# Packed copies of the leftover rows for four inverse transforms, and a new order of work

## The chip, the cores and the metric

One core of a Trainium2 chip runs the kernel as a single launch. The metric is the device time of one execution in microseconds (us). The core has five engines with instruction queues of their own: TensorE (PE in the profile, its weight loads PEld), VectorE (DVE), ScalarE (ACT), GpSimd (POOL) and SyncE (SP), which here issues nearly all DMAs. Queues run in order, and they wait for each other by semaphores.

## The reference

x has 2048 rows of 640 numbers in bf16. It is normalized by rows, and two branches are added to it: a two-dimensional Fourier filter, and a two-layer MLP with gelu.

```
xn = layernorm(x)                                  # (1, 2048, 640)
A  = irfft2(rfft2(xn) * (w_r + 1j * w_i))          # over rows and columns
h  = gelu(xn @ w1 + b1)                            # 640 -> 1536
B  = h @ w2 + b2                                   # 1536 -> 640
out = x + A + B
```

## The kernel before

The 2048 rows are 16 chunks (c = 0 to 15) of 128 rows; row p*16 + c is partition p of chunk c. The program first lists all steps with their buffers, and then places them by two texts written into the file: ORDER, which gives each step its engine and its place in that engine's queue, and SLOTS, which gives each buffer its slot. The method sync() derives the semaphore waits from the buffers. So the order is fixed ahead and nothing is decided on the chip. The first matmuls of the MLP and of the filter are mixed on TensorE, and the second MLP matmuls fill the places where the filter waits.

The steps, by the names in ORDER:

- Loads on SP: x0 to x14 (rows), w1_hj (ten pieces), w2_0 and w2_1 (halves of w2), W.. (sixteen large and two small pieces of the filter weights into the tile Wf, all on one semaphore), g, e, m, n, i, h (tables).
- Layernorm of chunk c: st, ag, then sq and rs or ve and rs, then nm, which writes the normalized chunk. sq uses a square root on ACT; table0 and table1 load the tables for the root and for gelu.
- Transposes into xnT: tp (TensorE) and tc (copy) for chunks 0 to 3, td (transposing DMA on SP) for the others. Chunk 0 is normalized in two parts, nm0 and nm0.3. b1mm and b1cp turn the bias b1 into a column.
- MLP, first layer: h{block}.{column block}.{first of the inner pieces}, gelu in ge. Second layer: k for chunks 1, 2, 4, 5, 7, 8, 10, 11, whose sum with x + b2 is put aside by kk; l for the others, which adds into the bank of the last step. xs adds b2 to x.
- Filter, way there: f1 and f2 fold the columns, G and gx transform over the rows (first half), b0 to b5 with xb transform over the columns (groups of 3, 3, 2, 3, 3 and 2), c with y finish the rows in 32x32 tiles, m and z multiply by the filter.
- Filter, way back: d and u (32x32 tiles), vt0 to vt15 (transposing DMAs on SP into XV), e0 to e5 (the same groups), yo, y2 and yf (unfolding), fin (last transform over the rows) and os (sum with what was put aside), out (stores).

A folded quarter of the columns has 160 rows here: 128, and 32 leftover. width() lists the matmuls of one group of n chunks: 4n with 128 rows of weights, then 4n with the 32 leftover rows of the four quarters, each in a row group of its own. In e0 to e5 the weights come from XV, 128 columns that lie 16 elements apart; in b0 to b5 they lie side by side. b, c, d and e all use PSUM banks 0 to 3, so that each of these groups waits until the one before it is copied out.

The lines of the profile: L410 is every matmul, L420 and L421 are copies on ACT and DVE, L405 loads, L559 td, L705 vt, L764 y2, L769 yf, L796 kk, L806 os, L813 out. The diff touches sync(), the tables of constants at L243 to L250, ORDER, SLOTS, the pools at L400 and the loop over the groups at L753.

Of the kernel before, what the change touches and what calls it, by code (L numbers as in the profile page):

```python
# [107 lines left out]
class Plan:  # L108
# [58 lines left out]
    def sync(self):  # L167
# [77 lines left out]
SUMS = 2  # L245
KEEP = (1, 2, 4, 5, 7, 8, 10, 11)
# [5 lines left out]
sp:x0 dve:warm0 act:bias1 pool:id0 pool:wpad dve:eps5 pool:id1 pe:idle0 sp:x1 act:table0 pool:xbpad2a pool:mhalf pool:xbpad0a pool:xbpad0b  # L252
pool:xbpad1b sp:w1_00 pool:xbpad1a pool:xbpad2b sp:w1_01 sp:w1_02 dve:st0.0 sp:x2 dve:st0.1 sp:w1_03 dve:st1.0 sp:w1_04 dve:ag0 dve:st1.1 sp:w1_10
act:sq0 dve:rs0 dve:ag1 sp:w1_11 dve:nm0 act:sq1 pe:b1mm dve:nm0.3 act:table1 sp:w1_12 dve:rs1 pe:tp0.3 dve:nm1 pe:tp0.0 sp:w1_13 pe:idle1 dve:tc0.0
pe:tp1.0 sp:w1_14 dve:f10.1 pe:h0.0.0 dve:f10.0 sp:x4 pe:h0.1.0 act:tc1.0 pe:h0.0.1 pe:h0.1.1 sp:x6 dve:f20.11 pe:h0.0.2 act:tc0.3 dve:f20.00
pe:h0.1.2 pe:h1.1.0 sp:g act:b1cp pe:h1.1.1 pe:h1.1.2 sp:x8 pe:h1.0.0 dve:st3.0 pe:h1.0.1 pe:h1.0.2 sp:x10 dve:st3.1 pe:h0.0.3 pe:h1.0.3 sp:x12
pe:h1.1.3 dve:ag3 dve:st2.0 pe:h0.0.4 pe:h0.1.3 dve:ve3 pe:h1.0.4 act:ge0.1 dve:st2.1 pe:h0.3.0 pool:rs3 pe:h1.1.4 act:ge1.0 pe:h0.2.0 dve:ag2
act:ge0.0 pe:h0.3.1 dve:ve2 pe:h0.1.4 act:ge1.4 dve:nm3 pe:h0.2.1 pool:rs2 pe:h0.2.2 act:ge0.3 dve:f20.10 pe:h1.3.0 act:ge1.1 pe:h1.3.1 dve:f20.01
pe:h0.3.2 act:ge1.2 dve:nm2 pe:tp3.0 pe:h1.3.2 dve:f11.0 pe:h1.3.3 act:tc3.0 pe:h1.3.4 dve:f11.1 pe:h0.3.3 pe:tp2.0 act:ge0.2 dve:st5.0 pe:h0.2.3
# [36 lines left out]
pe:h6.0.0 sp:vt12 act:ge6.10 pe:h6.0.3 pe:l3.0.6 act:ge6.0 pe:l3.384.0 pe:l3.384.3 pe:l3.384.6 pe:l3.384.9 pe:l0.0.0 pe:e0 pe:l0.0.3 act:yo0.0
dve:yo0.1 pe:l0.0.6 pe:l0.0.9 dve:y20.1 pe:e1 dve:y20.0 dve:yf0.0 pe:l0.384.0 act:yo1.0 pe:l0.384.3 dve:yf0.1 pe:l0.384.6 act:yo1.1 pe:l0.384.9
# [33 lines left out]
def bass_parallel_sum__spectral_gfnet__dense_activation_gelu__prompt_kernel(  # L331
# [20 lines left out]
    K = Plan(nc)  # L352
    with ExitStack() as es:
# [60 lines left out]
        def pe(name, lst, **kw):  # L414
            return K.op(name, "pe", mms(lst), **kw)
# [431 lines left out]
```

## Time and profile before

| what | value |
|---|---|
| three runs, median (lowest to highest) | 149.14 us (148.47 to 150.26) |
| the profiled execution, its own time | 148.87 us |
| its span, first to last instruction | 147.5 us |
| SP: issue of one transposing DMA into XV | 1.26 to 2.26 us |
| transposing DMA into XV, issue to landing | 2.6 to 4.5 us, median 2.8 |
| stores (160 KB), issue to landing | 1.8 us, median |
| HBM read and written | 10.92 MB and 2.62 MB |

What a run takes beyond its span, 1.37 us in the profiled one, lies before the first and after the last instruction. The profile gives busy times by engine and by line. A row of instructions has the engine, the line, the operation, the tile written and the tiles read, the shapes, the count, the total busy time, the mean in ns, and the idle time of the engine ahead of them with what ended it. A matmul's duration includes its way through the array, so the matmuls of one group overlap, and their durations add up to more than the group takes. A row of the timeline merges neighbouring instructions of the same form: start, length, engine, and the idle time ahead in brackets.

### The profile page before, as it was taken

Reading aid. Unit: us, or ns where it says so; the run is one execution under the profiler, and the core shown is the slowest. Engines: PE = TensorE matmul, PEld = TensorE weight load, DVE = VectorE, ACT = ScalarE, POOL = GpSimd, SP = SyncE. Lnnn points to the kernel's source line nnn. Section 1 sums busy time; section 2 is a strip of 40 time slices with the busy share of each in tenths; the row PEclk is TensorE's granted clock in tenths of the full one; section 3 lists DMA queues with packets and bytes.
Section 4 is the critical chain, followed back from the end, with each engine's and each line's share of the span. In section 5 each row is a group of like instructions: output and inputs, shape, how many; then the busy total and the mean of one; then the engine's idle time right before and its main releaser. Section 6 shows DMA issues by size and latency. Waiting matters only on the chain.

```text
span 147.5 us, 4149 instructions
## 1 busy us (share of the span) xinstructions
PE 141.7 (96%) x1751; PEld 99.8 (68%) x1760; DVE 114.7 (78%) x264; ACT 79.3 (54%) x149; POOL 7.2 (5%) x24
## 2 busy tenths in 40 slices
PE   7999999999999999999999999999899999999993
PEld 7899898886478867455364434446686786667882
DVE  2999999999997555798988999410488789296993
ACT  3659998979755734577795767655242102300000
POOL 2030204112000000000000000000000000000000
PEclk9999999999999999999999999999999999999999
DMA  4999869887999899000007685669001022012225
GB/s 135 306 354 408 142 141 343 145 101 137 293 155 160 221 201 266 16 4 0 7 0 57 126 118 99 103 131 94 2 0 49 0 78 102 5 44 89 89 93 178
DMA packets 29226, 18.40 MB, mean 125 GB/s; under 512 B 20248, under 2 KB 27928, under 8 KB 29080
## 3 DMA queue, kind: packets, MB, share of 16 engines
q1 hardware_dynamic: 29184, 18.14, 54.2%
q8 instruction: 14, 0.23, 0.6%
q14 instruction: 4, 0.03, 0.1%
q10 hardware_dynamic: 24, 0.00, 0.0%
HBM read 10.92 MB, written 2.62 MB: 92 GB/s over the span
## 4 chain that ended last, share of the span: by engine, by line
PE 86%; DMA 4%; ACT 3%; DVE 2%; SPq 2%; issue 1%
PE ps L410 85%; DMA XV<-U 2%; SPq L705 2%; ACT Xb L420 2%; DMA X<-in_A_x_dram 2%; DVE U L521 1%; ACT U L420 1%; PE ps L567 1%; ACT gT L639 0%; DVE T L553 0%; DVE W L806 0%; DVE mv L523 0%; DVE rstd L527 0%
## 5 line engine op out<-in xcount | busy, mean ns | idle before, releaser
L410 PE MATMUL ps<-W,gT 128*128 128x256 bf16 (+3 forms) x396 | 59.3, 296 | 0.0
L410 PE MATMUL ps<-xnT,W 128*128 128x256 bf16 (+2 forms) x411 | 55.5, 286 | 1.2 <-issue 1.1
L410 PEld LDWEIGHTS ps<-W,gT 128*128 128x128 bf16 x396 | 36.9, 98 | 15.4 <-issue 1.2
L410 PEld LDWEIGHTS ps<-xnT,W 128*128 128x128 bf16 x420 | 34.5, 98 | 16.0 <-issue 2.8
L639 ACT ACTIVATE gT<-ps,b1col 128x256 bf16<-128x256 f32 (+2 forms) x84 | 37.6, 524 | 10.3 <-PE ps L410 10.0
L420 ACT ACTIVATE Wf<-ps 128x960 bf16<-128x960 f32 (+1 forms) x8 | 6.7, 869 | 19.2 <-PE ps L410 15.7
L521 DVE BATCH_NORM_STATS2 U<-X 128x6 f32<-128x320 bf16 x32 | 14.1, 473 | 2.1 <-DMA X<-in_A_x_dram 2.1
L420 ACT ACTIVATE T<-ps 128x644 bf16<-128x644 f32 (+2 forms) x17 | 9.3, 580 | 4.7 <-PE ps L410 4.7
L796 DVE TENSOR_TENSOR xnT<-ps,X 128x384 f32<-128x384 f32 (+1 forms) x16 | 7.6, 486 | 4.8 <-PE ps L410 4.8
L806 DVE TENSOR_TENSOR W<-ps,xnT 128x384 bf16<-128x384 f32 (+1 forms) x16 | 7.5, 485 | 4.7 <-PE ps L410 4.5
L420 ACT ACTIVATE XV<-ps 128x1280 bf16<-128x1280 f32 (+1 forms) x8 | 9.6, 1202 | 2.0 <-PE ps L410 2.0
L421 DVE CAST Wf<-ps 128x960 bf16<-128x960 f32 (+1 forms) x4 | 4.3, 1073 | 7.1 <-PE ps L410 7.1
L584 DVE TENSOR_TENSOR T<-T 128x128 bf16<-128x128 bf16 (+1 forms) x32 | 8.9, 315 | 0.1
L806 DVE TENSOR_TENSOR W<-ps,X 128x384 bf16<-128x384 f32 (+3 forms) x17 | 7.6, 465 | 1.7 <-PE ps L410 1.6
L410 PE MATMUL ps<-Wf,htab 128*128 128x384 bf16 (+3 forms) x33 | 8.6, 296 | 0.0
L410 PE MATMUL ps<-getab,XV 32*128 32x160 bf16 (+1 forms) x128 | 7.5, 242 | 0.5 <-DMA XV<-U 0.5
L420 ACT ACTIVATE Xb<-ps 128x960 bf16<-128x960 f32 x5 | 6.2, 1260 | 3.4 <-PE ps L410 3.4
L410 PEld LDWEIGHTS ps<-getab,XV 32*128 32x128 bf16 (+1 forms) x128 | 6.7, 146 | 1.7 <-DMA XV<-U 0.8
L420 ACT ACTIVATE U<-ps 128x512 bf16<-128x512 f32 (+2 forms) x13 | 5.3, 475 | 4.4 <-PE ps L410 4.4
L699 DVE TENSOR_TENSOR T<-T 128x644 bf16<-128x644 bf16 x16 | 7.3, 487 | 0.2
L410 PE MATMUL ps<-EB,XV 32*128 32x160 bf16 (+1 forms) x128 | 7.2, 232 | 0.2 <-ACT Xb L420 0.2
L532 POOL TENSOR_TENSOR rstd<-ve,mhalf 128x2 f32<-128x2 f32 (+1 forms) x8 | 6.1, 758 | 26.6 <-DVE ve L531 26.6
(56 smaller groups left out, 124.6 us busy)
## 6 DMA issues: line engine op xcount, KB each, us to landing
out_dram<-W SPq DMA_DIRECT2D x15, 160.0 KB, 1.8
X<-in_A_x_dram SPq DMA_DIRECT2D x7, 320.0 KB, 5.8
W<-in_B_w_dram SPq DMA_DIRECT2D x10, 192.0 KB, 4.7
W<-in_B_w_dram SPq DMA_DIRECT2D x2, 960.0 KB, 7.0
Wf<-in_A_w_r_dram SPq DMA_DIRECT2D x7, 160.5 KB, 5.5
Wf<-in_A_w_i_dram SPq DMA_DIRECT2D x7, 160.5 KB, 3.8
gtab<-c_G SPq DMA_DIRECT2D x1, 512.0 KB, 7.5
htab<-c_H SPq DMA_DIRECT2D x1, 512.0 KB, 6.1
```

The lines of the kernel that those rows point to most:

```text
L410: ins = e.matmul(o_, lhsT=lw, rhs=rh, start=st, stop=sp_, skip_group_check=True)
L420: return e.activation(dst(), src(), ACT.Copy)
L421: return e.tensor_copy(dst(), src())
L521: K.op(f"st{c}.{h}", "dve", lambda e, _, c=c, h=h: e.bn_stats(stats[:, c, 6 * h:6 * h + 6], view(X, c * D + H2 * h, [[1, H2]])), reads=[B_ ...
L532: K.op(f"rs{c0}", "pool", lambda e, _, a=a, b=b: e.tensor_tensor(out=rstd[:, a:b], in0=ve[:, a:b], in1=mhalf[:, a:b], op=ALU.pow), reads=[ ...
L567: ins = e.transpose(psb(tps.slot, [[1, 512]]).bitcast(BF)[:, 128 * j:128 * j + 128], xnv(n, 128 * j, [[1, 128]]), ident)
L584: ring_ops.append(K.op(f"f2{pair}.{k}{i}", "dve", lambda e, _, op=op, x1v=x1v, xfv=xfv, o_=o_, o0=o0, o1=o1, w=w: e.tensor_tensor(out=xfv( ...
L639: K.op(f"ge{bi}.{fc}", "act", lambda e, _, c0=c0, nt=nt, fc=fc, f0=f0, hps=hps: e.activation(gT[:, fc, 128 * c0:128 * (c0 + nt)], psb(hps. ...
L699: return e.tensor_tensor(out=rows, in0=rows, in1=view(TT, TB.slot * 4 * KP + r * KP, [[2 * KP, 2], [1, KP]]), op=op)
L705: K.op(f"vt{q}", "sp", lambda e, _, q=q, qq=qq, U=Us[pair]: e.dma_start_transpose(XV[:, :, 128 * q:128 * q + 128], uv(U, D * qq, [[1, D]]) ...
L796: K.op(f"kk{c}.{o0}", "dve", lambda e, _, kps=kps, c=c, home=home, o0=o0, w=w: e.tensor_tensor(out=home[:, o0 // 128:(o0 + w) // 128], in0 ...
L806: K.op(f"os{c}.{o0}", "dve", lambda e, _, c=c, os_=os_, fps=fps, o0=o0, w=w, kept=kept, home=home if kept else None: e.tensor_tensor(out=( ...
```

## The change

Three things change. First, for the groups 2 to 5 (NEAR) a copy, xr, gathers the leftover rows of the group's n chunks out of XV into a tile T with the 128 columns side by side, and the leftover matmuls of e2 to e5 read their weights there. The copies are ready to run when the last vt has landed; xr2 and xr4 are placed on ACT, xr3 and xr5 on DVE. There are three slots; xr5 takes that of xr2 and so follows e2. The other e matmuls stay.

Second, a step no longer waits by semaphore for table0 or table1 when it runs on the same engine as they do.

Third, ORDER and SLOTS are new throughout. Steps change places in every queue, and some change engines: xb4.1 goes from ACT to DVE, gx7.0 and several y and yo from DVE to ACT. e2 and e3 change places: e0, e1, e2, e3, e4, e5 instead of e0, e1, e3, e2, e4, e5.

The sizes, the matmuls, the loads and the other copies are the same.

```diff
-            o.waits = [d for d in set(o.deps) if d.dma or d.eng != o.eng or o.eng != "pe"]
+            o.waits = [d for d in set(o.deps) if d.dma or d.eng != o.eng or o.eng != "pe" and d.name[:5] != "table"]
...
+NEAR = (2, 3, 4, 5)
...
-        p_yo, p_y2, p_yf, p_os = [Pool(k, n) for k, n in (("yo", 2), ("y2", 1), ("yf", 2), ("os", 4))]
+        p_yo, p_y2, p_yf, p_os, p_xr = [Pool(k, n) for k, n in (("yo", 2), ("y2", 1), ("yf", 2), ("os", 4), ("xr", 3))]
...
-            pe(f"e{gi}", lambda c0=c0, n=n, eps_=eps_: width(
-                eps_.slot, n, lambda i, g, p0, k: part(XV, p0, k, 2048 * g + c0 + i, [[16, 128]]), getab),
-                reads=B_v + [B_ge], writes=[eps_])
+            xr = K.buf(f"xr{gi}", p_xr) if gi in NEAR else None
+            if xr:
+                K.op(f"xr{gi}", "act dve", copy(lambda c0=c0, n=n, xr=xr: view(TT, 384 * xr.slot, [[128, n], [1, 128]]),
+                     lambda c0=c0, n=n: view(XV, 2048 * 4 + c0, [[1, n], [16, 128]])), reads=B_v, writes=[xr])
+            pe(f"e{gi}", lambda c0=c0, n=n, eps_=eps_, xr=xr: width(
+                eps_.slot, n, lambda i, g, p0, k: part(TT, p0, k, 384 * xr.slot + 128 * i, [[1, 128]]) if xr and g == 4 else part(XV, p0, k, 2048 * g + c0 + i, [[16, 128]]), getab),
+                reads=B_v + [B_ge] + ([xr] if xr else []), writes=[eps_])
```

Of ORDER, one queue at a time, the stretches that matter below (old, then new):

```
start, PE    old  b1mm tp0.3 tp0.0 idle1 tp1.0 h0.0.0 h0.1.0 h0.0.1 h0.1.1 h0.0.2 h0.1.2 h1.1.0
             new  tp0.3 b1mm tp0.0 idle1 tp1.0 h0.1.0 h0.1.1 h0.0.0 h0.0.1 h0.0.2 h1.0.0
start, ACT   old  sq1 table1 tc1.0 tc0.3 b1cp          new  sq1 table1 b1cp tc1.0 tc0.3
start, DVE   old  rs0 ag1 nm0 nm0.3 rs1 nm1            new  rs0 ag1 nm0.3 nm0 rs1 nm1
SP           old  td11 W12n bias2 W00m w2_1 W02p W02n e W01n td12 td14 td15 td13 W11p W03n W10p m ...
             new  td9 td8 bias2 w2_1 W11p W13n m W12p W03n W10m e W03p W10p W00p W02n W01n W12n W11n td12 td15 td14 td13 ...
PE           old  G10 h5.3.3 h5.1.0 h5.1.3 h4.8.0 h4.8.3 h4.9.0 k2.0.0 k2.0.3 k1.0.6
             new  h5.0.3 G11 h5.5.0 k1.0.6 k1.0.9 G10 k2.0.0
PE           old  b4 h5.6.0 h5.6.3 h5.7.0 h5.7.3 b3    new  b4 k4.0.0 k4.0.3 h5.6.0 b3
DVE          old  ... y2.0 m1.1 m1.0 z1.0 m0.1 z1.1 m0.0 m3.1 xb3.0
             new  ... y2.0 kk5.384 m1.1 m0.1 m1.0 z1.0 z1.1 xb4.1 m3.1 m0.0 xb3.0
ACT          old  u0.1 u1.1 ge5.10 u1.0 u2.0           new  u0.0 u1.0 ge5.11 u1.1 u0.1 u3.0
SP           old  vt2 vt3 vt1 vt7 vt0 vt6 vt4 vt5 vt8 vt9 vt11 vt10 vt14 vt15 vt13 vt12
             new  vt1 vt2 vt3 vt6 vt0 vt7 vt4 vt5 vt11 vt9 vt10 vt8 vt14 vt15 vt12 vt13
PE           old  d3.0 h6.4.0 h6.4.3 h6.10.0 h6.10.3 k8.0.9 l3.0.0 h6.11.0 h6.11.3 l3.0.3 h6.0.0 h6.0.3 l3.0.6
                  l3.384.0 l3.384.3 l3.384.6 l3.384.9 l0.0.0 e0
             new  d3.0 h6.11.3 h6.10.0 h6.8.0 h6.8.3 l3.0.0 h6.10.3 l3.0.3 l3.0.6 h6.0.0 l3.0.9 h6.4.0 h6.4.3 h6.0.3
                  l3.384.0 l3.384.3 l3.384.6 l0.0.0 e0
PE           old  e1 l0.384.0 .3 .6 .9 fin0.0 fin0.384 l3.0.9 e3 ...
             new  e1 l0.384.0 .3 .6 .9 fin0.384 l0.0.9 fin0.0 e2 k11.0.0 .3 .6 .9 l6.0.0 fin2.0 fin1.0 fin3.384 ...
DVE          new  xr3 yo0.1 y20.0 y20.1 yf0.1 yf0.0 os0.384 y21.1 y21.0 xr5 os0.0 yf1.0 yf1.1 kk11.0
ACT          new  ge6.0 xr2 yo0.0 xr4 yo1.0 yo1.1 yo2.0 yo2.1
```

More of the change, by code (lines that the diff above doesn't have):

```diff
@@ L251 @@
 ORDER = """
[L252 to L259, printed above, removed]
@@ new lines @@
+pe:h6.8.3 pe:l3.0.0 sp:vt15 act:ge6.8 pe:h6.10.3 act:ge6.11 pe:l3.0.3 act:ge6.10 sp:vt12 pe:l3.0.6 pe:h6.0.0 pe:l3.0.9 sp:vt13 pe:h6.4.0 pe:h6.4.3
+pe:h6.0.3 act:ge6.4 pe:l3.384.0 pe:l3.384.3 act:ge6.0 pe:l3.384.6 dve:xr3 act:xr2 pe:l0.0.0 pe:e0 pe:l0.0.3 dve:yo0.1 act:yo0.0 pe:l3.384.9 pe:l0.0.6
+act:xr4 dve:y20.0 pe:e1 dve:y20.1 pe:l0.384.0 dve:yf0.1 act:yo1.0 pe:l0.384.3 dve:yf0.0 pe:l0.384.6 act:yo1.1 pe:l0.384.9 pe:fin0.384 pe:l0.0.9
+dve:os0.384 pe:fin0.0 dve:y21.1 pe:e2 dve:y21.0 pe:k11.0.0 act:yo2.0 dve:xr5 pe:k11.0.3 dve:os0.0 act:yo2.1 pe:k11.0.6 dve:yf1.0 sp:out0.0 pe:k11.0.9
@@ new lines @@
+bps0:0 xb1:1 bps1:0 xb2:2 bps2:0 xb3:0 bps3:0 xb4:1 bps4:0 xb5:3 bps5:0 Y0:1 Y1:0 Y2:2 Y3:3 Y4:5 Y5:4 Y6:0 Y7:1 T0:1 T1:0 T2:1 T3:0 T4:0 T5:1 T6:0
+T7:1 U0:0 U1:1 U2:3 U3:2 U4:1 U5:0 U6:3 U7:2 cps0_0:0 cps0_1:0 dps0_0:0 dps0_1:0 cps1_0:0 cps1_1:0 dps1_0:0 dps1_1:0 cps2_0:0 cps2_1:0 dps2_0:0
+dps2_1:0 cps3_0:0 cps3_1:0 dps3_0:0 dps3_1:0 yo0:0 y20:0 yf0:0 eps0:0 os0:0 fps0_0:6 fps0_384:5 os1:2 kps1_0:4 kps1_384:5 fps1_0:1 fps1_384:4 os2:1
+kps2_0:6 kps2_384:7 fps2_0:0 fps2_384:7 yo1:1 y21:0 yf1:1 eps1:0 os3:0 fps3_0:4 fps3_384:7 os4:3 kps4_0:5 kps4_384:7 fps4_0:4 fps4_384:0 os5:0
@@ new lines @@
+kps5_0:6 kps5_384:5 fps5_0:1 fps5_384:7 yo2:0 y22:0 yf2:0 eps2:0 xr2:0 os6:2 fps6_0:6 fps6_384:6 os7:1 kps7_0:5 kps7_384:7 fps7_0:3 fps7_384:1 yo3:1
+y23:0 yf3:0 eps3:0 xr3:2 os8:3 kps8_0:6 kps8_384:7 fps8_0:2 fps8_384:6 os9:0 fps9_0:7 fps9_384:1 os10:1 kps10_0:5 kps10_384:6 fps10_0:5 fps10_384:5
+yo4:0 y24:0 yf4:1 eps4:0 xr4:1 os11:2 kps11_0:5 kps11_384:7 fps11_0:1 fps11_384:0 os12:0 fps12_0:2 fps12_384:0 os13:3 fps13_0:5 fps13_384:4 yo5:0
+y25:0 yf5:1 eps5:0 xr5:0 os14:2 fps14_0:3 fps14_384:4 os15:1 fps15_0:2 fps15_320:6 fps15_480:3
```

128 lines of the change are left out of this document (62 added, 66 removed).

## The prediction, made before the changed kernel was run

> **What bounds the kernel now.** I read the page first, then the busy time by stretches, then the chain of work in order of time.
>
> ```profile
> span 147.5 us, 4149 instructions
> ...
> PE 141.7 (96%) x1751; PEld 99.8 (68%) x1760; DVE 114.7 (78%) x264; ACT 79.3 (54%) x149; POOL 7.2 (5%) x24
> ```
>
> ```profile
> 5.60:60.00 54.40, 54.32 (x644) 43.64 (x646) 47.61 (x134) 41.04 (x84) 6.06 (x8) 1.00 0.94 220
> 60.00:103.90 43.90, 41.96 (x683) 21.11 (x688) 31.96 (x55) 29.36 (x55) 0.15 (x2) 1.00 0.43 62
> 103.90:145.00 41.10, 41.06 (x389) 30.96 (x389) 32.03 (x64) 6.74 (x8) 0.00 (x0) 1.00 0.15 54
> ```
>
> ```profile
> 100.19 3.65 DMA XV<-U
> ...
> 103.89 41.09 PE ps L410 x375
> ...
> 145.00 0.33 DVE W L806
> ```
>
> In the second fence the first number after the stretch is its length, then come the busy times of PE, PEld, DVE, ACT and POOL. TensorE is the bound: it is idle for 0.08 us between 5.6 and 60, for 1.94 us between 60 and 103.9, and for 0.04 us of the last 41. The granted clock is 1.00 throughout. So only three things can shorten the kernel: less TensorE time per matmul, less of those 1.94 us, or a shorter start or end. A new order alone can give little, and any wait it opens on TensorE is paid in full. The chain shows what starts the last stretch: the last transposing DMA of XV, landing at 103.84.
>
> **The change part by part.** *Leftover rows.* Each of the transforms e0 to e5 has 4n matmuls with 128 rows of XV as weights and 4n with 32 leftover rows (n chunks in the group). In both, 128 weight columns are read 16 elements apart. The transforms b0 to b5 have the same shapes with neighbouring columns, so they are the yardstick.
>
> ```profile
> L410 PEld LDWEIGHTS ps<-getab,XV 128*128 128x128 bf16 x64 | 5.1, 144 | 1.2 <-DMA XV<-U 0.8 <-ACT Wf L420 0.2
> ...
> L410 PE MATMUL ps<-getab,XV 32*128 32x160 bf16 x64 | 2.5, 250 | 0.0
> ...
> L410 PE MATMUL ps<-EB,XV 32*128 32x160 bf16 x64 | 2.2, 231 | 0.0
> ...
> L410 PEld LDWEIGHTS ps<-getab,XV 32*128 32x128 bf16 x64 | 1.6, 148 | 0.5
> ...
> L410 PEld LDWEIGHTS ps<-EB,XV 32*128 32x128 bf16 x64 | 1.0, 92 | 0.8
> ```
>
> ```profile
> 110.09 1.36 PE L410 MATMUL ps<-getab,XV 128*128 128x160 bf16 x24
> ```
>
> ```profile
> 125.27 1.02 PE L410 MATMUL ps<-getab,XV 128*128 128x160 bf16 x16
> ```
>
> ```profile
> 63.40 1.31 PE L410 MATMUL ps<-EB,XV 128*128 128x160 bf16 x24
> ```
>
> ```profile
> 81.74 0.96 PE L410 MATMUL ps<-EB,XV 128*128 128x160 bf16 x16
> ```
>
> A leftover load takes 148 ns strided and 92 ns packed. The change packs those of e2 to e5: 2+3+3+2 = 10 chunks, 40 loads. Were every load on TensorE's path, that would be 40 x 56 ns = 2.2 us; that is one end, and nothing is the other. The whole groups decide between them: 24 matmuls take 1.36 strided against 1.31 packed, 16 take 1.02 against 0.96. So one delay of about 0.05 us per group is visible, and the same for two chunks as for three; the rest lies behind running matmuls. Four groups x 0.05 = **-0.20 us**. The 128-row loads stay strided (144 ns).
>
> The Trainium skill (TensorE: Matmul & The Clock Gate, Part 3, The mechanism) says that a weight load overlaps running matmuls only where its row group differs. By that rule each later round of four leftover loads, which returns to the same row groups, would be exposed, so 1+2+2+1 = 6 rounds x 56 ns = 0.34 us would be gained instead of 0.20. The trace does not agree: three chunks lose no more than two.
>
> *The copies.* xr2 and xr4 go to ACT and xr3 and xr5 to DVE, 384 or 256 elements each, with a 16-element source step.
>
> ```profile
> L420 ACT ACTIVATE Wf<-ps 128x960 bf16<-128x960 f32 x5 | 4.7, 969 | 12.6 <-PE ps L410 12.6
> ...
> L764 DVE TENSOR_TENSOR Wf<-Wf 128x960 bf16<-128x960 bf16 x8 | 5.1, 652 | 0.1
> ...
> L806 DVE TENSOR_TENSOR W<-ps,xnT 128x384 bf16<-128x384 f32 x8 | 4.4, 551 | 2.8 <-PE ps L410 2.7
> ...
> L420 ACT ACTIVATE xnT<-ps 128x640 bf16<-128x640 bf16 x3 | 2.1, 703 | 0.3 <-PE ps L567 0.2
> ...
> L420 ACT ACTIVATE xnT<-ps 128x256 bf16<-128x256 bf16 x1 | 0.4, 378 | 0.0
> L421 DVE COPY xnT<-ps 128x384 bf16<-128x384 bf16 x1 | 0.4, 358 | 0.0
> ```
>
> No row copies with that step within SBUF; the nearest give 0.36 to 0.55 us on DVE and 0.38 to 0.70 on ACT, and I take 0.4 and 0.5. The Trainium skill (VectorE: DVE Perf Modes, the TRN2 errata) has (224 + 384)/1.2 GHz, an estimated 0.51 us, for ACT's larger one; no run here shows it. xr2 and xr3 run beside e0, xr4 behind yo0.0; ACT sat idle for 12.6 us before its Wf copies, so those cost nothing. xr5 is the tight one. It stands in DVE's queue ahead of os0.0, yf1.0 and yf1.1, and fin3.384 on TensorE waits for yf1.1. From the end of e1: two ACT copies (1.9), two y2 (1.3), xr5 (0.4), os0.0 (0.55), two yf (1.3), 5.5 us in all. TensorE's work there in the new order is four 256-column triples, e2, five 384-column triples, one more of these for l0.0.9, and four single matmuls: 1.3 + 1.0 + 2.4 + 0.5 + 0.6 = 5.8 us. It covers xr5 by 0.3 us, so 0; without that cover up to +0.4.
>
> *The wait before e0.*
>
> ```profile
> 95.37 1.42 ACT L420 ACTIVATE U<-ps 128x512 bf16<-128x512 f32 x4 [0.86 <-PE ps L410]
> ```
>
> ```profile
> 84.96 4.69 SPq L705 DMA_TRANSPOSE XV<-U  x3
> 90.44 3.10 SPq L705 DMA_TRANSPOSE XV<-gtab  x2
> ...
> 96.23 6.22 SPq L705 DMA_TRANSPOSE XV<-U  x4
> ```
>
> ```profile
> 95.20 2.33 PE L410 MATMUL ps<-xnT,W 128*128 128x512 bf16 x10
> ...
> 103.89 0.29 PE L410 MATMUL ps<-getab,XV 128*128 128x160 bf16 x1 [0.45 <-DMA XV<-U]
> ```
>
> After d3.0, ACT empties its banks, and then SP issues the last four transposes (6.22 us of issue) and the last lands 3.65 us after its own issue began. The new order keeps d3.0, u7.0, u6.0 and four transposes in that sequence, and d3.0 has the same TensorE work ahead of it (0.05 us more). So e0 starts when it did. SP's first transpose is now vt1, which needs u0.1, the fourth evacuation in ACT's queue instead of the third, some 0.7 us later (half of the 1.42 above, which are two evacuations); SP was idle from 89.65 to 90.44, and that takes it up with nothing left, so 0, and any more delay there goes to e0. Between d3.0 and e0 the new order has two more 512-column matmuls (2.33 us for ten, so 0.22 each) and one 256-column triple less (0.32 by columns): **-0.11 us** of work taken out of the stretch behind the wait. Ends: 0, and the whole 0.45.
>
> *The wait for Xb.*
>
> ```profile
> 64.76 2.37 ACT L420 ACTIVATE Xb<-ps 128x960 bf16<-128x960 f32 x2 [0.48 <-PE ps L410]
> ```
>
> ```profile
> 67.19 1.32 PE L410 MATMUL ps<-EB,XV 128*128 128x160 bf16 x24 [0.21 <-ACT Xb L420]
> ```
>
> b3 waited 0.21 us because ACT made both halves of xb4. Now DVE makes xb4.1, ready about 1.3 us after b4 if DVE is free. **-0.21 us**. But DVE has m1.1, m0.1, m1.0, z1.0 and z1.1 queued ahead; if these hold it, the wait returns up to 0.5 larger.
>
> *The start.*
>
> ```profile
> 6.67 0.98 ACT L420 ACTIVATE xnT<-ps 128x640 bf16<-128x640 bf16 x2
> 7.53 0.19 ACT L510 ACTIVATE b1col<-ps 128x12 f32<-128x12 f32 x1
> ```
>
> ```profile
> 6.53 1.85 PE L410 MATMUL ps<-xnT,W 128*128 128x128 bf16 x30
> ```
>
> b1cp (0.19) now precedes tc1.0, which ends 0.1 later, at 7.47 (6.67 + 0.70 + 0.1). The first matmul on chunk 1 is now TensorE's 16th of these instead of its 19th. At (1.85 - 0.22)/29 = 0.056 us each it is due at 7.37: a wait of 0.1 us, with the semaphore **+0.13**. Ends: 0 and +0.3. nm0.3 now precedes nm0, but tp1.0 still waits for nm1, so that gains nothing.
>
> *Loads and transposes on SP.*
>
> ```profile
> 33.50 0.55 SPq L405 DMA_DIRECT2D Wf<-in_A_w_r_dram  x1
> 34.08 0.58 SPq L405 DMA_DIRECT2D W<-in_B_w_dram  x1
> ...
> 37.31 6.82 SPq L559 DMA_TRANSPOSE xnT<-T  x3
> ```
>
> ```profile
> W<-in_B_w_dram SPq DMA_DIRECT2D x2, 960.0 KB, 7.0
> ```
>
> ```profile
> 42.05 1.63 PE L410 MATMUL ps<-W,gT 128*128 128x384 bf16 x9
> ```
>
> td12 to td15 now stand behind some seven more loads of 0.6 us, so about 4 us later; block 6 reads them only near 80 us, so 0. The Wf loads end earlier; 0. w2_1 moves the other way: two loads fewer ahead of it, but its first reader k1.0.6 (third triple of the last row, 43.0) has 6,000 columns less ahead of it, 2.5 us: 40.5. Issued near 32.9 and landing after 7.0, w2_1 is there at 39.9: 0, with 0.6 us to spare.
>
> *Waits on the activation tables* are dropped. The first gelu runs long after its table is in; 0.
>
> *Everything else in the order* moves work between queues whose margins I estimate at 0.1 to 0.3 us against evacuations of 0.4 to 1.2 us. As TensorE repays no wait, I put +0.15, with ends 0 and +0.8.
>
> Sum, against the profiled execution's own 148.87 us: 148.87 - 0.20 - 0.11 - 0.21 + 0.13 + 0.15 = 148.63, **148.6 us**. That execution lies 0.27 below the median of the runs (149.14).
>
> **The rivals.** (1) *The change does nothing that counts*: the strided reads were hidden, or each gain ends at the next wait. Then the gains drop out: 148.87 + 0.13 + 0.15 = 149.15. For it: only 0.05 us per group is exposed. Against: it shows in two- and three-chunk groups alike. (2) *The order fills TensorE's holes*: if most of the 1.94 us goes, 148.87 - 0.2 - 1.7 = 147.0. Against: the 0.45 before e0 hangs on a chain that did not move, and much of the rest is a gap at each switch from 32-row tiles back to 128 rows, as in the row below, and the order holds as many of these groups as before.
>
> ```profile
> 80.75 1.03 PE L410 MATMUL ps<-xnT,W 128*128 128x512 bf16 x4 [0.16 <-issue]
> ```
>
> (3) *w2_1 is late, slower*: twelve Wf loads now follow it closely and share the DMA engines. From a landing of 7.6 us on, k1.0.6 waits and every further us is a us: at 9.0 us 148.6 + 1.4 = 150.0, at 10 us 151.0. Against: fewer loads queue ahead of it.
>
> **How the numbers follow.** Forecast 0.55, rival 1 0.26, rival 2 0.09, rival 3 0.10. A measurement of this kernel tells about 1% (1.5 us) from no change. Faster by over 1% is below 147.65: most of rival 2, 0.08. Slower is above 150.63: the worse half of rival 3, 0.06. The rest is 0.86. The range leaves out rival 2 and most of rival 3: 147.8 to 149.7; its upper part is the +0.8 of the order's margins.
>
> **What would show it.** In the changed profile the e groups packed should take 1.31 and 0.96 us, and the mean of the 32-row matmuls should fall from 250 towards 238. The XV wait before e0 should be near 0.35, the one for Xb before b3 gone, and TensorE should wait about 0.1 near 7.4. Wrong would be the e groups unchanged, a wait of TensorE on W near 40, on DVE's Xb near 67, or on Wf in the last 40 us.

## The result, and the profile after

| | median | lowest to highest | ratio to before |
|---|---|---|---|
| before | 149.14 us | 148.47 to 150.28 | |
| after | 154.82 us | 152.73 to 155.41 | 1.034 (1.030 to 1.039) |

The changed kernel is 3.4% slower where no change was forecast. The profiled execution took 155.0 us with a span of 153.7, against 148.87 and 147.5 before. The intervals here and below are at 95% and leave out runs over 1.5% above the fastest of the same kernel, so all runs are given where that matters. Of the page of the changed kernel, its span, its engines and the row of the granted clock in 40 slices:

```profile
span 153.7 us, 4169 instructions
...
PE 146.1 (95%) x1760; PEld 100.8 (66%) x1760; DVE 112.4 (73%) x261; ACT 83.3 (54%) x156; POOL 6.8 (4%) x24
...
PEclk9999999999965999999999999999999999999999
```

TensorE is busy 4.4 us longer than before, with the same matmuls. Not all of that is time lost: the profile of before lacks nine of the 1760 matmul records, all of one form (its row, then that of the changed kernel):

```profile
L410 PE MATMUL ps<-xnT,W 128*128 128x512 bf16 x111 | 27.0, 380 | 1.2 <-issue 1.1
```

```profile
L411 PE MATMUL ps<-xnT,W 128*128 128x512 bf16 x120 | 30.4, 384 | 0.0
```

Eight gaps on TensorE, 1.2 us in all, go with the missing records; the profiles with all 1760 show at most one such gap. The other 3.2 us are the matter here. Two slices, the 12th and the 13th, have a lower granted clock, near 42 to 50 us. The chain of work shows what stands there (start, length, what):

```profile
33.38 10.97 DMA W<-in_B_w_dram
44.39 24.66 PE ps L411 x301
...
106.67 3.63 DMA XV<-U
110.34 37.48 PE ps L411 x345
```

A load of W, w2_1, holds TensorE up until 44.39. From e0 on (110.34) nothing is longer than before, where that stretch began at 103.89. The timeline of TensorE and then its busy time by stretches (start:end, length, busy times of PE, PEld, DVE, ACT and POOL, clock, DMA share, GB/s; at a DMA share of 1 or a little more the DMA engines are busy all the time):

```profile
40.65 0.81 PE L411 MATMUL ps<-xnT,W 128*128 128x512 bf16 x3
44.39 2.10 PE L411 MATMUL ps<-W,gT 128*128 128x384 bf16 x6 [2.93 <-DMA W<-in_B_w_dram]
46.29 0.74 PE L411 MATMUL ps<-gtab,T 128*128 128x128 bf16 x5
46.82 2.13 PE L411 MATMUL ps<-W,gT 128*128 128x384 bf16 x6
```

```profile
41.46:43.40 1.94, 0.00 (x1) 0.00 (x0) 1.24 (x4) 0.06 (x1) 0.00 (x0) 1.00 1.20 200
43.50:44.39 0.89, 0.00 (x0) 0.00 (x0) 0.00 (x0) 0.00 (x0) 0.00 (x0) 0.50 1.02 194
44.39:50.30 5.91, 5.91 (x23) 3.14 (x24) 2.23 (x6) 1.24 (x1) 0.00 (x0) 0.50 1.30 203
50.50:60.00 9.50, 9.50 (x121) 7.92 (x119) 4.86 (x6) 6.93 (x11) 0.00 (x0) 1.00 0.75 192
```

k1.0.6 waits 2.93 us. After 2 us of this wait the clock falls to half and stays there for 6.8 us, 5.91 of them with work: six matmuls of 384 columns take 2.10 us instead of the 1.14 of the kernels below. There is a second, smaller wait on W at k1.0.0, the first reader of w2_0:

```profile
28.50 0.65 PE L411 MATMUL ps<-W,gT 128*128 128x384 bf16 x3 [0.66 <-DMA W<-in_B_w_dram]
```

Together 0.66 + 2.93 + 5.91/2 = 6.5 us, which is what the span lost against a kernel without these three (147.2, below). Why is w2_1 late? The answers for its load alone, before and after (one issue of that form: its length in ns three times, its start; then issue to landing):

```profile
L405 SPq DMA_DIRECT2D W<-in_B_w_dram x1: 583/583/583, 34.1 to 34.1; - x1
...
DMA to landing us min/median/max: 8.0/8.0/8.0
```

```profile
L406 SPq DMA_DIRECT2D W<-in_B_w_dram x1: 429/429/429, 33.4 to 33.4; - x1
...
DMA to landing us min/median/max: 11.0/11.0/11.0
```

It is issued 0.7 us sooner and lands 2.2 us later. What follows it on SP has changed:

```profile
33.38 0.43 SPq L406 DMA_DIRECT2D W<-in_B_w_dram  x1
33.85 1.62 SPq L406 DMA_DIRECT2D Wf<-in_A_w_i_dram  x2
...
42.30 1.28 SPq L406 DMA_DIRECT2D Wf<-in_A_w_i_dram  x2
43.62 6.88 SPq L560 DMA_TRANSPOSE xnT<-T  x2
```

Ten us of loads stand behind w2_1, where before there were 2.6 us of them (34.66 to 37.31) and then transposes.

### The profile page after: what moved, and what is told of

Same layout as the page of the kernel before. It is cut to its first block, busy times and chain, and to the rows that moved or that the text cites. A ratio compares the mean times of both kernels' runs of the same rounds, so it can differ in the third digit from the quotient of the medians.

```text
span 153.7 us, 4169 instructions
## 1 busy us (share of the span) xinstructions
PE 146.1 (95%) x1760; PEld 100.8 (66%) x1760; DVE 112.4 (73%) x261; ACT 83.3 (54%) x156; POOL 6.8 (4%) x24
## 4 chain that ended last, share of the span: by engine, by line
PE 64%; DVE 16%; DMA 12%; SPq 2%; POOL 2%; issue 1%; ACT 1%; DVEq 0%
PE ps L411 63%; DMA W<-in_B_w_dram 7%; DVE U L522 7%; DMA XV<-U 2%; DVE T L585 2%; DVE T L554 2%; DVE T L581 2%; SPq L560 2%; POOL rstd L533 2%; DMA X<-in_A_x_dram 1%; DMA out_dram<-W 1%; ACT gT L640 1%; DVE W L811 1%; DVE mv L524 1%; PE ps L568 0%
## 5 line engine op out<-in xcount | busy, mean ns | idle before, releaser
L411 PE MATMUL ps<-W,gT 128*128 128x384 bf16 (+3 forms) x396 | 62.6, 303 | 3.6 <-DMA W<-in_B_w_dram 3.6
L411 PE MATMUL ps<-xnT,W 128*128 128x256 bf16 (+2 forms) x420 | 58.6, 289 | 0.0
L421 ACT ACTIVATE XV<-ps 128x1280 bf16<-128x1280 f32 (+2 forms) x9 | 10.0, 1122 | 8.8 <-PE ps L411 8.6
L585 DVE TENSOR_TENSOR T<-T 128x512 bf16<-128x512 bf16 (+1 forms) x32 | 9.2, 312 | 4.5 <-PE ps L411 4.4
L811 DVE TENSOR_TENSOR W<-ps,X 128x256 bf16<-128x256 f32 (+3 forms) x17 | 7.5, 465 | 2.3 <-DMA out_dram<-W 1.6
L411 PE MATMUL ps<-Wf,htab 128*128 128x256 bf16 (+3 forms) x33 | 8.5, 296 | 0.0
L554 DVE TENSOR_SCALAR T<-X,mv,rstd 128x640 bf16<-128x640 bf16 (+2 forms) x17 | 7.1, 432 | 1.3 <-POOL rstd L533 1.2
L581 DVE TENSOR_TENSOR T<-T 128x640 bf16<-128x640 bf16 x16 | 7.4, 485 | 0.2
L769 DVE TENSOR_TENSOR Wf<-Wf 128x960 bf16<-128x960 bf16 (+1 forms) x12 | 6.9, 596 | 0.7 <-ACT Wf L421 0.6
L422 DVE CAST Xb<-ps 128x960 bf16<-128x960 f32 x4 | 5.0, 1245 | 2.9 <-PE ps L411 2.8
```

Of the source, the lines that this page charges most:

```text
L411: ins = e.matmul(o_, lhsT=lw, rhs=rh, start=st, stop=sp_, skip_group_check=True)
L421: return e.activation(dst(), src(), ACT.Copy)
L422: return e.tensor_copy(dst(), src())
L554: norm = K.op(f"nm{c}" if not a else f"nm{c}.3", "dve", lambda e, _, c=c, n=n, a=a, b=b, xnv=xnv: e.tensor_scalar(out=xnv(n, a, [[1, b - a ...
L581: K.op(f"f1{pair}.{k}", "dve", lambda e, _, k=k, op=op, xnv=xnv, x1v=x1v: e.tensor_tensor(out=x1v(H2 * k, [[D, 2], [1, H2]]), in0=xnv(0, 0 ...
L585: ring_ops.append(K.op(f"f2{pair}.{k}{i}", "dve", lambda e, _, op=op, x1v=x1v, xfv=xfv, o_=o_, o0=o0, o1=o1, w=w: e.tensor_tensor(out=xfv( ...
```

## The experiments

**Theory**: the order of the loads makes w2_0 and w2_1 late. TensorE pays the waits, and then half a clock because it stood idle. **Rivals**: k1.0.6 simply stands too early; the clock falls for another reason; the copies or another part of the order cost the time.

Every ratio is to the kernel before in the same group of runs: its medians were 149.32 us (experiments 1 to 4), 148.66 (5 to 7) and 149.15 (8 to 10 and the control).

**1. Both groups of loads moved back**

```diff
 SP  ... x14
-    W00n w2_0 W10n ... bias2 w2_1 W11p W13n m W12p W03n W10m e W03p W10p W00p W02n W01n W12n W11n td12 td15 td14 td13 W00m ...
+    w2_0 W00n W10n ... bias2 w2_1 e td12 td15 td14 td13 W11p W13n m W12p W03n W10m W03p W10p W00p W02n W01n W12n W11n W00m ...
```

> The changed kernel, with the twelve loads that SP issues right behind w2_1 (W11p W13n m W12p W03n W10m W03p W10p W00p W02n W01n, W12n, W11n; e stays) moved behind td13, and W00n moved from just ahead of w2_0 to just behind it. PE's, VectorE's and ScalarE's orders stay. Theory (the loads that follow w2_1 share the 16 DMA engines with it): w2_1, issued near 33.4, has landed by 39.5 to 41.5 instead of 44.4; k1.0.6 waits 0 to 0.3 instead of 2.93; without the idle time the granted clock stays at 1.00 through 40 to 50; 148.3 to 149.3 us. Rival (k1.0.6 simply stands too early, whatever follows w2_1): w2_1 lands at 43 or later, the wait stays over 2 us, 153 to 155. Rival (the copies or another part of the order cost the time): the wait goes, the time stays above 151.

148.57 us, ratio 0.996 (0.993 to 1.000), clock 1.00 in all ten runs. The whole loss is gone, with the copies, the dropped table waits and all compute orders of the change still in. So the load order is enough to explain it. In a later group of runs the same kernel was the control:

> The kernel of the first experiment once more (both groups of loads moved back), as the control of this group of runs: 148.2 to 149.0 us, within 0.5% of the kernel before, no wait on the weights of the second product over 0.3 us, clock 1.00.

148.93 us, 1.000 (0.997 to 1.002). Its timeline has k1.0.6 at 40.59 without a wait:

```profile
40.59 1.14 PE L411 MATMUL ps<-W,gT 128*128 128x384 bf16 x6
```

**2. The reader moved instead of the loads**

```diff
 PE  h5.5.0
-    k1.0.6 k1.0.9
     G10 k2.0.0 k2.0.3 h5.5.3 k4.384.0 k4.384.3 G12 G13
+    k1.0.6 k1.0.9
     k2.0.6
```
(with kk1.0 on VectorE moved along)

> The changed kernel with its order on SP untouched; on PE k1.0.6 and k1.0.9 (and on VectorE kk1.0) moved from ahead of G10 to just behind G13, so that TensorE has about 3 us of other work while w2_1 is under way. Theory (the late load costs only because k1.0.6 is due ahead of it, and the lowered clock only because TensorE stood idle): w2_1 still lands near 44, the wait on it is 0 to 0.6, the granted clock stays near 1.00, 149.2 to 150.2 us. Rival (the crowd of loads costs in itself, by other late transfers or a clock that falls for another reason): 152 us or more, with the half clock in the fifth slice of ten still there.

150.48 us, 1.010 (1.004 to 1.016); clock 1.00. That is just above the expected range, which had not counted a wait of k1.0.0. w2_1 still took 11.2 us and landed at 45.45, but only 0.42 of that was left as a wait, and k1.0.0 waited 1.14. The two waits, 1.56 us, make up nearly all of the 1.55 to 1.9 us by which it lies above experiment 1's two medians. So the crowd on the DMA engines costs next to nothing in itself; what counts is who waits.

**3. Work that nobody needs, in the wait**

```diff
 PE  h5.5.0
+    idle2          # 58 matmuls of 128 columns
     k1.0.6 k1.0.9 G10
```

> The changed kernel with 58 matmuls of 128 columns on the identity (about 3.1 us of work whose result nobody reads, in an idle slot of PSUM) put on PE just ahead of k1.0.6; nothing else moves. w2_1 is as late as before and TensorE does nothing useful until it lands, but it isn't idle. Theory (the lowered clock from 44.4 to 50.5 follows from the idle time and costs about 2.9 us): the clock is 0.99 to 1.00 throughout, 151.5 to 152.4 us. Rival (the clock falls for another reason, or its fall costs nothing that ends up on the path): the half clock stays, 154.3 to 155.5 us.

154.10 us, 1.031 (1.024 to 1.038). The clock stayed at 1.00 in all four runs, as expected, but the time missed the expectation by 2 us, since everything else was later. The loads' own scatter put w2_1 at 45.88 (11.5 us after its issue), so that k1.0.6 came 3.83 us late (3.40 of idle2 and 0.43 of wait) and k1.0.0 1.44; and 1.6 us were lost on a late store near the end (last section). By its time alone it decides nothing, so the question went to experiments 6 and 7.

**4. The new load order in the kernel before**

```diff
 SP  ... x14
-    w2_0 W10m W03p td6 ...
+    W00n w2_0 W10n td6 ...
...
-    bias2 W00m w2_1 W02p W02n e W01n td12 td14 td15 td13 ...
+    bias2 w2_1 W11p W13n m W12p W03n W10m e W03p W10p W00p W02n W01n W12n W11n td12 td14 td15 td13 ...
```

> The kernel before, with nothing of the change but the order of the loads on SP: W00n ahead of w2_0 and W10n behind it, and behind w2_1 the same twelve loads and e. No copies, and the orders of PE, VectorE and ScalarE those of before, so that k1.0.6 is due at 42.9. Theory (the crowd behind w2_1 makes it late): it lands at 43.5 to 45 instead of 42.1, k1.0.6 waits 0.5 to 2, and if that is long enough the clock falls too: 150.0 to 153.5 us. Rival (only the earlier place of k1.0.6 matters): w2_1 lands by 42.5 as before, 149.0 to 149.4 us.

152.34 us, 1.020 (1.015 to 1.026): the time came as expected, but not at the expected place. w2_1 took 9.0 us and nobody waited for it. The loss was at w2_0:

```profile
29.29 0.65 PE L410 MATMUL ps<-W,gT 128*128 128x384 bf16 x3 [2.37 <-DMA W<-in_B_w_dram]
```

```profile
26.90:29.29 2.39, 0.02 (x1) 1.00 1.05 138
30.00:33.30 3.30, 3.30 (x16) 0.50 1.01 179
```

(In stretches that show one engine, the figures are start:end, length, busy time of TensorE, clock, DMA share and GB/s.) 2.37 of wait and a stretch of 3.4 us at half clock (1.7) are the 4.0 us between this span (151.5) and that of before. Two of the four runs kept a clock of 1.00 and took 151.72 and 151.93; these were not profiled. So the load order costs time under the old compute order too. Here k1.0.6 is due later, at 42.9 plus what k1.0.0 lost.

**5. The changed kernel again, and one of its two moves undone**

> The changed kernel itself, unaltered, on the chip of this group of runs. It is here so that the loads' scatter from run to run can be told from the edits: 152.7 to 155.4 us as in its first runs, and a mean granted clock that takes steps of 0.011 (1.00, 0.989, 0.978), since each stretch at half clock is 3.4 us long and costs 1.7. If instead the clock varies without such steps, or does not go with the time, the half clock is no countable part of the loss.

155.38 us (154.74 to 156.07), two of the four runs above the expected range. The clock takes the steps: 0.989 in three runs, 0.978 in the slowest. In the first five runs of the changed kernel it was 1.00 in the run of 152.73, 0.989 at 154.64 and 154.82, and 0.978 at 155.0 and 155.41. The times of 0.989 and of 0.978 lie close together, so the count of stretches does not set the time alone; the waits scatter as well (1.22 and 3.14 us in this profile, 0.66 and 2.93 in the first).

```diff
 SP  ... x14
-    W00n w2_0 W10n
+    w2_0 W00n W10n
```

> The changed kernel with one move on SP: W00n from just ahead of w2_0 to just behind it. The twelve loads behind w2_1 stay. Theory (each load of the weights of the second product is delayed by what stands around it): the wait of k1.0.0 near 28 (0.67 us in the changed kernel's first profile, 1.1 to 1.4 in the two experiments that kept this order) goes, w2_1 is issued up to 1 us earlier, but still lands 10 us or more after its issue, so k1.0.6 still waits 2.5 to 4: 0.5 to 1.5 us below the changed kernel in the same group of runs. Rival (W00n counts for nothing, w2_0 is late for its own reasons): the wait near 28 stays over 0.5 us and the time is that of the changed kernel.

Median of ten runs 150.49. Six took 149.25 to 150.49 at a clock of 1.00, and over these the ratio is 1.009 (1.005 to 1.012); the other four took 154.12 to 155.47 at 0.978 to 0.989. The wait of k1.0.0 is gone. In the profile, of one of the six, w2_1 took 9.2 us from its issue, and

```profile
42.05 1.15 PE L411 MATMUL ps<-W,gT 128*128 128x384 bf16 x6 [1.05 <-DMA W<-in_B_w_dram]
```

A wait of 1.05 leaves the clock alone. The same order of loads thus gives a short wait in some executions, and in others presumably one long enough for the clock to fall; those were not profiled. I had expected w2_1 to take 10 us or more and a gain of 0.5 to 1.5 us; six runs gained nearly 5 us on the changed kernel's 155.38, the other four about what I had expected or nothing.

**6 and 7. A late load without a crowd, idle or kept busy**

```diff
 SP  bias2
-    w2_1
     e td12
+    w2_1
     td15 td14 td13
```
(to the kernel of experiment 1; experiment 7 also has idle2 ahead of k1.0.6)

> The first experiment's kernel (loads moved behind td13, 148.57 us), with w2_1 itself issued later, behind e and td12, so that it comes late with no crowd behind it. TensorE stands idle at k1.0.6 for some 3.5 to 5 us. Theory (idle time is followed by stretches of 3.4 us at half clock): one or two such stretches follow, 1.7 us lost in each, mean granted clock 0.978 to 0.989, and the time is 148.6 plus the idle time plus 1.7 to 3.4: 154 to 157 us. Rival (the clock falls because of the crowd on the DMA engines, not because of the idle time): the clock stays at 1.00, 152 to 153.6 us.

> As the run before (w2_1 late, no crowd), with 58 matmuls of 128 columns whose result nobody reads on PE just ahead of k1.0.6. Theory: the wait for w2_1 costs as much as in the run before, but TensorE is not idle long enough for the clock to fall: 1.00, and 1.7 to 3.4 us less than in the run before, 152 to 153.6 us. Rival (the half clock costs nothing on the path, or the clock falls all the same): within 0.7 us of the run before.

Idle 153.94 us, 1.034 (1.028 to 1.041), clock 0.989 in all four runs; kept busy 152.38, 1.023 (1.014 to 1.031), clock 1.00 in all four. The stretches of the idle one and the timeline of the busy one:

```profile
41.44:44.11 2.67, 0.01 (x1) 1.00 1.10 347
44.11:47.50 3.39, 3.39 (x14) 0.50 1.05 242
47.50:108.40 60.90, 60.67 (x936) 1.00 0.46 89
```

```profile
41.45 3.40 PE L411 MATMUL ps<-EB 128*128 128x128 bf16 x58
44.69 1.14 PE L411 MATMUL ps<-W,gT 128*128 128x384 bf16 x6
```

The clock falls behind an idle time with no crowd of loads behind w2_1, and doesn't fall when the same time is filled. The DMA engines are as busy in the one as in the other (share 1.10 in the idle time, 1.11 from 41.44 to 44.69 in the busy kernel), so it is not they that lower the clock. From k1.0.6 to e0 the idle kernel takes 108.44 - 44.11 = 64.33 us and the busy one 106.92 - 44.69 = 62.23; without the 0.27 that the idle one waits for XV the difference is 1.8, near the 1.7 of one stretch. The idle kernel stayed just under its expected range because w2_1, with nothing beside it, took only 5.2 us. By the medians the busy kernel is 1.6 us faster, a little under the expected 1.7 to 3.4: it came to k1.0.6 0.6 us later and lost 1.2 us near its end (last section).

**8. The other move undone alone**

```diff
 SP  ... x14
-    w2_0 W00n W10n
+    W00n w2_0 W10n
```
(to the kernel of experiment 1)

> The kernel of the first experiment with W00n put back ahead of w2_0; the twelve loads stay behind td13. It is the fourth corner of a square: neither moved back 155, only W00n moved back 150.5 (in 6 of 10 runs), both moved back 148.6. Theory (two separate delays of about 1 us and of 2 to 4): k1.0.0 waits 0.7 to 1.4 near 28, w2_1 is issued about 1 us later and lands 8 us or less after its issue, k1.0.6 waits under 0.5, the clock stays at 1.00: 149.3 to 150.3 us. Rival (the late w2_0 sets off the late w2_1): the wait of k1.0.6 is over 1.5 us, 151 or more.

150.43 us, 1.008 (1.005 to 1.011), clock 1.00. Just above the expected range, because k1.0.0 waits longer than expected; k1.0.6 waits little:

```profile
29.81 0.65 PE L411 MATMUL ps<-W,gT 128*128 128x384 bf16 x3 [1.89 <-DMA W<-in_B_w_dram]
43.01 1.15 PE L411 MATMUL ps<-W,gT 128*128 128x384 bf16 x6 [0.23 <-DMA W<-in_B_w_dram]
```

W00n, one load ahead of w2_0, is worth 1.5 to 1.9 us by itself. The square, with the issue-to-landing times of the two loads in the profiled executions:

| W00n ahead of w2_0 | twelve loads right behind w2_1 | w2_0 | w2_1 | time, median |
|---|---|---|---|---|
| yes | yes (the change) | 7.7, 8.4 | 11.0, 11.2 | 154.82, 155.38 |
| no | yes | 6.1 | 9.2 | 150.49 (four of ten runs at 154.12 to 155.47) |
| yes | no | 8.9 | 7.9 | 150.43 |
| no | no | 5.9, 6.1 | 7.6, 7.6 | 148.57, 148.93 |

The two do not add up. Part of that is the clock, which fell behind waits of 2.4 us and more and not behind shorter ones. Why w2_1 takes 2 us more in the changed kernel, where w2_0 was late as well, stays open: experiment 4 has the same order of loads, and w2_1 took 9.0 us there. Why W00n, a load of 150 to 160 KB, delays w2_0 by 1.6 to 2.8 us when it stands ahead stays open too.

**9. The copies taken out again**

```diff
-NEAR = (2, 3, 4, 5)
+NEAR = ()
...
-act:xr2 dve:xr3 act:xr4 dve:xr5
```
(in the kernel of experiment 1)

> The kernel of the first experiment without the four copies: the leftover rows of groups 2 to 5 are again loaded from where they lie, one strided weight load for each part, as in the kernel before. Same result, same order otherwise. Theory (the step of the change worth 0.05 us for each group): e2 to e5 take 0.04 to 0.06 us longer each, from the start of e0 to the last matmul 0.15 to 0.25 us more than in the control, 148.6 to 149.1 us. Rival (the copies cost as much on VectorE and ScalarE as they save on TensorE): the time from e0 to the last matmul is the control's within 0.05 us, or shorter.

148.88 us, 0.998 (0.995 to 1.000), against 148.93 for the control: the times can't tell them apart. The chains can, the control first:

```profile
103.60 37.48 PE ps L411 x348
```

```profile
103.78 37.66 PE ps L411 x343
```

The copies save 0.18 us between e0 and the last stores; in the eight profiles that have the copies and this order at the end, the stretch takes 37.47 or 37.48 us. The packed groups themselves took 0.97 us for two chunks and 1.32 for three in the changed kernel (116.53 to 117.50 and 123.18 to 124.50), close to the forecast 0.96 and 1.31. The changed kernel's groups show where from: a packed leftover load takes 92 ns, a strided one 148, and their matmuls 232 and 248; over all 64 matmuls that is a mean of 238, as forecast.

```profile
L411 PE MATMUL ps<-getab,T 32*128 32x160 bf16 x40 | 1.4, 232 | 0.0
...
L411 PE MATMUL ps<-getab,XV 32*128 32x160 bf16 x24 | 0.9, 248 | 0.0
...
L411 PEld LDWEIGHTS ps<-getab,T 32*128 32x128 bf16 x40 | 0.6, 92 | 0.3
L411 PEld LDWEIGHTS ps<-getab,XV 32*128 32x128 bf16 x24 | 0.6, 148 | 0.2
```

**10. A version that keeps the good parts**

```diff
-("os", 4)      os14:2  os15:1
+("os", 8)      os14:5  os15:4
...
 PE  l0.0.0
-    e0
     l0.0.3
+    e0
```
(to the kernel of experiment 1)

> The kernel of the first experiment with three small edits at the end: eight places instead of four for the output rows (the tile has the room), os14 and os15 put into places of their own so that os15.0 needn't wait for the store of out10, and e0 one step of three matmuls (0.49 us) later on PE, so that work stands in its wait for XV. Theory: the wait for XV goes from 0.65 to under 0.25, VectorE's wait for the store (0.62) goes, the last of it is worth 0.1: 147.8 to 148.3 us. Rival (e0 later makes e1 or the first stores late by as much; the last store's own time sets the end): within 0.2 of the control.

148.67 us (148.21 to 149.06), 0.996 (0.994 to 0.999) of before: a version that is ahead of both kernels, if by little. (Experiment 1's kernel was clear of 1 in its first group of runs and not in its second.) Against the control of its group (148.93) it is not clearly better, and the expected 147.8 to 148.3 us did not come. The wait for XV went, and its place was taken by one at e1, which waits for a copy of e0's result out of the PSUM banks:

```profile
104.08 1.43 PE L411 MATMUL ps<-getab,XV 128*128 128x160 bf16 x24
105.44 0.99 PE L411 MATMUL ps<-W,gT 128*128 128x256 bf16 x6
106.88 1.39 PE L411 MATMUL ps<-getab,XV 128*128 128x160 bf16 x24 [0.44 <-DVE Wf L422]
```

## Why the prediction was wrong

**What bounds the kernel**: right, and it carries the loss: "any wait it opens on TensorE is paid in full". It is paid more than in full.

**Loads and transposes on SP**: this is the step that failed. It said "Issued near 32.9 and landing after 7.0, w2_1 is there at 39.9: 0, with 0.6 us to spare." The due time was right (40.5; 40.59 in the control). It was issued at 33.38, half a microsecond later. The 7.0 was wrong by more. It is the median of two loads, w2_0 at 6.1 and w2_1 at 8.0 in the kernel before; with w2_1's own number the spare was already gone. And neither number belongs to the new order: w2_1 measured 11.0, and 7.9 once the twelve loads behind it were moved (experiment 8). W00n, put ahead of w2_0, was not priced at all: it cost a wait of 0.66 in the profile, and of 1.89 alone in experiment 8.

**Rival 3** had the place and the mechanism ("twelve Wf loads now follow it closely and share the DMA engines"). Its price was "every further us is a us", 151.0 at a landing of 10. From a landing of 11.0 that gives 152; measured was 155. Missing were the half clock behind the wait (2.95 us) and w2_0 (0.66). Its chance of 0.10 rested on the 7.0 and on "fewer loads queue ahead of it". The runs show that what is queued behind a load counts: with w2_0 at 6.1 us both times, w2_1 took 7.6 without the twelve loads behind it and 9.2 with them.

The Trainium skill (DMA: Bandwidth & Descriptors, Issuing engines are not separate DMA queues) says that DMAs run on the same 16 engines and interleave. These two times agree with it.

**Rival 2** had less room than it thought. Of the 1.94 us that TensorE seemed idle between 60 and 103.9, 1.2 are the eight gaps that go with the missing records of the profile before; the control has all 1760 records and none of these gaps. So "a gap at each switch from 32-row tiles back to 128 rows" was no hole that an order could fill.

**The rest of the sum** is borne out as a whole, in part by luck: with the two groups of loads moved back, the forecast of 148.6 meets 148.57 and 148.93. But the kernel before took 149.32 and 149.15 in the same groups of runs, so the gain was 0.75 or 0.2 us where the sum had 0.24, and only two of its parts were seen at their size:

- Leftover rows, -0.20: measured -0.18 (experiment 9).
- Copies at nothing: right, though three of the four take longer than my 0.4 and 0.5 us (0.74 and 0.89 on ScalarE, 0.85 and 0.38 on VectorE). TensorE is busy throughout the 37.48 us from e0 on, and the kernel without them is no shorter. The two on VectorE:

```profile
L422 DVE COPY T<-XV 128x384 bf16<-128x384 bf16 (+1 forms) x2 | 1.2, 616 | 9.1 <-DMA XV<-U 9.1
```

- The wait before e0, -0.11: not borne out. It should have come to 0.35; it measured 0.21 and 0.45 in the changed kernel, 0.65 and 0.47 in experiment 1, against 0.45 before. That is scatter, and experiment 10 shows that filling the wait moves it to e1.
- The wait for Xb, -0.21: gone, as said; the changed kernel's waits of TensorE have no row for Xb.

```profile
PE ps L411 <- DMA W<-in_B_w_dram: 3.6, 2, 2.9
PE ps L411 <- DVE EB L427: 1.0, 1, 1.0
PE ps L411 <- DMA XV<-U: 0.2, 1, 0.2
PE ps L568 <- DVE T L554: 0.2, 1, 0.2
PE ps L411 <- issue: 0.2, 1, 0.2
```

- The start (+0.13): the wait expected near 7.4 us does not show in the changed kernel's profile, where TensorE is busy without a gap from 6.5 to 10. The order's margins (+0.15) and the table waits were not tested one by one.
- One thing was overlooked at the end: os15 takes the place of os10 and so waits for the store out10.0, 0.43 us of VectorE in the changed kernel (0.62 in the control). Before, it waited for no store there. About a quarter of a microsecond of it reaches the end of the control: VectorE's last sum ends 0.62 us after TensorE's last matmul there, against 0.36 before and in experiment 10, where the wait is gone.

```profile
150.71 0.95 DVE L811 TENSOR_TENSOR W<-ps,X 128x320 bf16<-128x320 f32 x3 [0.43 <-DMA out_dram<-W]
```

## What to carry to other kernels

When a load is moved, take its own time and not a median of its form, and ask what now stands just ahead of it and just behind it: 12 loads behind a 960 KB load and one ahead of another cost 6 us here, with not a byte more moved. Price a wait of TensorE like those profiled here (2.4 to 3.1 us) at its length plus up to 1.7 us for each of one or two stretches of half clock that may follow it. And spare time of 0.6 us is none against a landing that took 7.5 to 11.5 us by what stood around the load. Count the records of a profile before its gaps are taken for idle time.

## What the runs showed of the hardware

The half clock comes in whole stretches of 3.4 us: one in the kernels of experiments 4 and 6, two in a row (6.8) in the changed kernel's first profile, one in its second. Idle times of 2.4 to 3.1 us brought it on, those of 1.05, 1.14, 1.44 and 1.89 did not. It can start after the idle time is over: in experiment 4 work resumed at 29.29 and the clock fell near 30.0. In the traces' clock records the changes lie whole multiples of 3.413 us apart: 37.55 us at full clock and then 6.83 at half in the changed kernel (11 and 2 times), 23.89 and 3.41 in experiment 4 (7 and 1). So the windows seem to run on regardless of the work, and it matters how an idle time falls into them: in the changed kernel 2.0 us of the wait lay ahead of the fall. Nor is it shown that every long wait brings it on: a run of the changed kernel (152.73 us) and two of experiment 4 lost 2.4 to 3.6 us against the medians of before at a clock of 1.00, though where they waited is not known. The Trainium skill (TensorE: Matmul & The Clock Gate, Part 1, What's actually happening) has a free-running window of 3413 ns and two clocks, full and half. The traces agree with the window and the two values; that an idle window of about 3.4 us is needed, as its table has it, they do not show: 2.37 us were enough.

A load of instructions seems to delay a store. In the traces' DMA records the last 16 KB piece of the program is fetched at a fixed place in the order of work (38.1 us after the start of e0 in the control and in the changed kernel), and takes 0.9 to 1.7 us. In the control it starts at 141.73, and the store issued at 141.69 (out10.0) lands after 2.38 us instead of 1.75. In experiment 7, with 58 matmuls more in the program, it starts at 138.07 and meets out6.0, which takes 3.5 (and the piece ahead of it, at 123.98, meets out1.0, which takes 3.65); there the output place is needed at once, and TensorE waits:

```profile
141.11 0.83 PE L411 MATMUL ps<-W,gT 128*128 128x256 bf16 x6 [0.75 <-DVE W L812]
142.37 0.34 PE L411 MATMUL ps<-Wf,htab 128*128 128x384 bf16 x1 [0.43 <-DVE W L812]
```

The two kernels with idle2 lost 1.2 and 1.6 us in such waits. That the fetch is the cause was read from the times alone; it was not tested by itself.
